# Loading the residual rows of x from SyncE instead of GpSimd, and widening a zero fill, in an attention-and-gate kernel

## Chip, cores, metric

The kernel runs on one core of one Trainium2 chip. The metric is device time in microseconds (us) of one launch, the median of several executions. Engines are named as the profile names them: PE is TensorE's matmuls, PEld its weight loads, DVE is VectorE, ACT is ScalarE, POOL is GpSimd, SP is SyncE; "SPq" or "ACTq" is the instruction queue of that engine, from which it also issues transfers. The landing of a transfer is the moment when its data is in place; PSUM is the memory that TensorE writes its results to. All runs here are recorded as of the same (fast) state; a "slow start" or "slow execution" below is something else, a matter of the first 10 us.

## The reference, cut to what matters

```
x  = A_x                                    # 2048 rows x 640, bf16
xn = layernorm(x)
q  = xn @ wq                                # 32 heads of 192
k, v = the last 512 rows of the caches
s  = softmax(q k^T / sqrt(192)) v @ wo      # 2048 x 640, summed over 32 heads
g  = silu((sigmoid(xn @ w_gate) * (xn @ w_up)) @ w_down)
return x + s * g
```

The kernel first computes the gate `g` and keeps it. Then it runs attention in 8 groups of 4 heads (0 to 7), each over four blocks ("units") of 512 rows, and sums the projections of the groups in `acc`. So that the end is cheap, `acc` is turned into `acc * g + x` already after group 6, on GpSimd; group 7 adds only its own part times `g`.

## The kernel before: the parts that count

The start: order of the first loads. The fill writes zeros that the gate-weight load then overwrites. It is a delay: ScalarE's load has to wait for it.

```
nc.vector.memset(wg_sb[:, 0, 0:2 * P], 0.0)      # 256 columns = 128 words of 32 bits
load_x(0, 1)                                     # SyncE, 160 KB
load_x(1, 1)                                     # SyncE, 160 KB
load_f(nc.scalar, wg_sb, wg_r, 0, 4, 0, 3)       # ScalarE, gate weights, 384 KB
load_f(nc.sync, wg_sb, wg_r, 0, 4, 3, NCD)       # SyncE, 256 KB
load_f(nc.sync, wu_sb, wu_r, 0, 4, 0, 3)         # SyncE, up weights, 384 KB
load_x(2, 1)
# ... cut: the rest of the loads
dummy(17)                                        # matmuls on zeros, to get TensorE going
```

The projection of one 128-row block, where the rows of x are loaded:

```
def project(u, q, k, out_eng=None, add=nc.vector, two=True):
    g, b = u // NB, u % NB                       # group, block of 512 rows
    t = b * TQ + q                               # block of 128 rows
    for turn in range(2 if two else 1):
        # ... cut: 12 matmuls of oT[u] and wo into a PSUM bank, then a yield
    # ... cut: groups 0 and 7
        nc.vector.tensor_tensor(cols(acc[:, t, :]), res, cols(acc[:, t, :]), ALU.add)
    if g == NG - 2:                              # group 6
        x_sb = fin.tile([P, D], BF16, name="row")            # pool fin has 2 buffers
        nc.gpsimd.dma_start(x_sb[:], xf[t * P:(t + 1) * P, :])
        nc.gpsimd.tensor_tensor(acc[:, t, :], acc[:, t, :], gate[:, t, :], ALU.mult)
        nc.gpsimd.tensor_tensor(acc[:, t, :], acc[:, t, :], x_sb[:], ALU.add)
    yield
```

The driver interleaves attention values of unit u with projections of unit u - 2. SyncE issues, in program order, the transposes of the next group's keys (`turn_keys`), those of each unit's output (`turn_out`, o_st to oT, four per unit) and the wo loads. GpSimd issues the loads of the next group's wq, keys and values (`load_values`, into the single tile `vbuf`).

The softmax here doesn't subtract the row's maximum and nothing guards it: scores larger than these inputs give would overflow.

## Time and profile before

| | before |
|---|---|
| time, 3 runs | 922.06 us (921.71 to 922.27) |
| TensorE busy | 914.1 of 919.2 us |
| GpSimd busy | 134.6 us |
| GpSimd waits for rows of x | 16.1 us in 14 waits |

The prediction below shows the busy table, TensorE's waits, the chain at the start and the two timelines.

### The profile page before, as it was taken

The numbers are of one execution on the slowest core, as the hardware profiler recorded it, in microseconds if no ns is written. First come the engines' busy times: TensorE is split into PE (matmuls) and PEld (weight loads), VectorE is DVE, ScalarE is ACT, GpSimd is POOL, SyncE is SP. The second block draws the span as 40 slices with busy tenths as digits, with TensorE's granted clock in tenths as the row PEclk, the third lists the DMA queues.
The fourth block names the chain that finished last, engine by engine and source line by source line (L and its number), as shares of the span: only waits on it lengthen the run. The fifth ranks groups of instructions, "written<-read, shape, count | busy, mean of one in ns | idle before, by whom it ended". The sixth has DMA issues, their size and how long they took to land.

```text
span 919.2 us, 24974 instructions
## 1 busy us (share of the span) xinstructions
PE 914.1 (99%) x11333; PEld 622.8 (68%) x11333; DVE 492.5 (54%) x989; ACT 302.3 (33%) x332; POOL 134.6 (15%) x159
## 2 busy tenths in 40 slices
PE   9999999999999999999999999999999999999998
PEld 4445455465868686867676777777776767686875
DVE  6462522444646464646555555545564646464667
ACT  4222222255141424242333333242424151515150
POOL 1000100001002000200020011001100111174733
PEclk9999999999999999999999999999999999999999
DMA  9820330115434334342425162515251615253435
GB/s 320 164 44 1 89 87 1 43 62 88 78 63 111 81 64 77 94 98 45 95 85 107 36 104 79 113 31 109 66 108 46 113 61 95 62 120 104 88 84 135
DMA packets 172106, 79.35 MB, mean 86 GB/s; under 512 B 149952, under 2 KB 167568, under 8 KB 172000
## 3 DMA queue, kind: packets, MB, share of 16 engines
q1 hardware_dynamic: 164640, 55.85, 31.1%
q0 software_dynamic: 5808, 20.52, 7.8%
q8 instruction: 88, 1.44, 0.7%
q10 hardware_dynamic: 1552, 1.39, 0.5%
q14 instruction: 18, 0.15, 0.1%
HBM read 39.45 MB, written 2.62 MB: 46 GB/s over the span
## 4 chain that ended last, share of the span: by engine, by line
PE 99%; DMA 1%; DVE 0%; SPq 0%; DVEq 0%; issue 0%
PE bank L517 22%; PE bank L446 21%; PE bank L468 19%; PE bank L428 18%; PE bank L251 8%; PE bank L263 6%; PE bank L293 3%; PE bank L394 1%; DMA wu_sb<-in_B_w_up_dram 1%; PE bank L552 0%; DVE o_sb L498 0%; DVE gate L503 0%; SPq L162 0%; PE bank L235 0%; SPq L167 0%; DVEq L654 0%
## 5 line engine op out<-in xcount | busy, mean ns | idle before, releaser
L432 ACT ACTIVATE E<-bank 128x1024 bf16<-128x1024 f32 x256 | 255.3, 1022 | 456.5 <-PE bank L428 456.4
L446 PE MATMUL bank<-xnT,wq_sb 64*128 64x512 bf16 x1800 | 226.4, 376 | 0.0
L517 PE MATMUL bank<-wo_sb,oT 64*128 64x320 bf16 x2688 | 205.2, 296 | 0.0
L428 PE MATMUL bank<-qT,kT 64*128 64x512 bf16 x1536 | 200.7, 376 | 0.0
L468 PE MATMUL bank<-vbuf,E 64*128 64x193 bf16 x4096 | 195.3, 243 | 0.0
L468 PEld LDWEIGHTS <-E 64*128 64x128 bf16 x4096 | 178.8, 94 | 10.2 <-issue 0.3
L517 PEld LDWEIGHTS <-oT 64*128 64x128 bf16 (+1 forms) x2892 | 163.2, 94 | 30.7 <-issue 0.3
L453 DVE CAST qT<-bank 128x1024 bf16<-128x1024 f32 x90 | 110.2, 1224 | 128.5 <-PE bank L446 128.5
L446 PEld LDWEIGHTS <-wq_sb 64*128 64x128 bf16 x1800 | 106.1, 100 | 87.0 <-issue 0.4
L428 PEld LDWEIGHTS <-kT 64*128 64x128 bf16 x1536 | 88.1, 94 | 73.5
L481 DVE TENSOR_TENSOR o_st<-bank,rden 128x768 bf16<-128x768 f32 x128 | 122.6, 957 | 4.4
L532 DVE TENSOR_TENSOR acc<-bank,acc 128x640 f32<-128x640 f32 x96 | 79.0, 823 | 20.2 <-PE bank L517 20.2
L118 POOL DMA_DIRECT2D vbuf<-in_A_v_cache_dram x28 | 21.1, 753 | 311.0 <-PE bank L468 308.1
L451 DVE COPY seen<-bank 128x2 f32<-128x2 f32 x90 | 14.3, 159 | 79.1 <-PE bank L446 79.1
L480 DVE RECIPROCAL rden<-bank 128x4 f32<-128x4 f32 x128 | 23.4, 182 | 60.6 <-PE bank L468 59.6
L263 PE MATMUL bank<-wd_sb,hT 128*128 128x512 bf16 (+1 forms) x384 | 52.8, 299 | 0.0
L263 PEld LDWEIGHTS <-hT 128*128 128x128 bf16 x384 | 29.7, 98 | 23.1
L251 PE MATMUL bank<-xnT,wg_sb 128*128 128x512 bf16 x180 | 44.7, 379 | 0.0
L251 PE MATMUL bank<-xnT,wu_sb 128*128 128x512 bf16 x180 | 44.7, 379 | 0.0
L257 DVE TENSOR_TENSOR hT<-bank,sig 128x512 bf16<-128x512 f32 x36 | 24.8, 690 | 37.1 <-ACT sig L254 37.1
L254 ACT ACTIVATE sig<-bank 128x512 bf16<-128x512 f32 x36 | 21.5, 597 | 55.8 <-PE bank L251 52.7
L97 POOL DMA_DIRECT2D wq_sb<-in_A_wq_dram x7 | 6.3, 900 | 210.7 <-PE bank L446 210.7
(51 smaller groups left out, 406.1 us busy)
## 6 DMA issues: line engine op xcount, KB each, us to landing
wo_sb<-in_A_wo_dram SPq DMA_DIRECT2D x7, 960.0 KB, 5.6
wq_sb<-in_A_wq_dram POOLq DMA_DIRECT2D x7, 960.0 KB, 6.1
k_st<-in_A_k_cache_dram POOLq DMA_DIRECT2D x14, 384.0 KB, 5.6
vbuf<-in_A_v_cache_dram POOLq DMA_DIRECT2D x28, 192.0 KB, 3.5
row<-in_A_x_dram POOLq DMA_DIRECT2D x16, 160.0 KB, 2.7
oT<-o_st SPq DMA_TRANSPOSE x128, 3.4
x_sb<-in_A_x_dram SPq DMA_DIRECT2D x3, 640.0 KB, 9.4
wd_sb<-in_B_w_down_dram SPq DMA_DIRECT2D x1, 1920.0 KB, 14.4
```

The lines of the kernel that those rows point to most:

```text
L251: nc.tensor.matmul(bank[k][:, half, 0:r1 - r0], lhsT=w[:, c, f * P:(f + 1) * P], rhs=xnT[:, b, c, r0:r1], start=(c == 0), stop=(c == NCD - 1))
L257: nc.vector.tensor_tensor(hT[b][:, f, r0:r1], bank[k][:, 1, 0:r1 - r0], sig[:, 0:r1 - r0], ALU.mult)
L263: nc.tensor.matmul(wide(k)[:, d0:d1], lhsT=hT[b][:, f, q * P:(q + 1) * P], rhs=wd_sb[:, f, d0:d1], start=(f == 0), stop=(f == NF - 1))
L293: nc.tensor.matmul(bank[k][:, half, :], lhsT=xcT[:, c, t * P:(t + 1) * P], rhs=w[:, c, fg * FT:(fg + 1) * FT], start=(c == 0), stop=(c == ...
L428: nc.tensor.matmul(bank[k][:, i, :], lhsT=kT[r, pr, j, c * P:(c + 1) * P], rhs=q[r, pr * DJ + j, :], start=(j == 0), stop=(j == DJ - 1))
L432: nc.scalar.activation(E[u, pr][:, c, :, :], bank[k][:], AF.Exp, scale=scale_qk)
L446: nc.tensor.matmul(bank[k][:, half, :], lhsT=wq[r, c, col:col + DJ * (P - 1) + 1:DJ], rhs=xnT[r, b, c, :], start=(c == 0 and not second), ...
L453: nc.vector.tensor_copy(qT[u][:, 2 * m:2 * m + 2, :], bank[k][:])
L468: nc.tensor.matmul(o4[:, q, 0:DH + 1], lhsT=e[r, c, h % 2, q * P:(q + 1) * P], rhs=vbuf[r, h, c, 0:DH + 1], start=(turn == 0 and qq == 0 a ...
L481: nc.vector.tensor_tensor(o_st[u][:, :, h * DH:(h + 1) * DH], o4[:, :, 0:DH], rden[:].to_broadcast([P, TQ, DH]), ALU.mult)
L517: nc.tensor.matmul(res[:, half, :], lhsT=oT[u][r, cc, q * P:(q + 1) * P], rhs=wo[r, cc, half * HD:(half + 1) * HD], start=(turn == 0 and c ...
L532: nc.vector.tensor_tensor(cols(acc[:, t, :]), res, cols(acc[:, t, :]), ALU.add)
```

## The change

Its intent: take 16 transfer issues off GpSimd and have each row in place before its sum is ready. The fill becomes 352 columns wide (176 words), so the gate-weight load starts a little later and leaves the x rows alone a little longer.

```
-        nc.vector.memset(wg_sb[:, 0, 0:2 * P], 0.0)
+        nc.vector.memset(wg_sb[:, 0, 0:352], 0.0)
...
         res = bank[k][:, :, 0:HD]
+        if g == NG - 2:
+            x_sb = fin.tile([P, D], BF16, name="row")
+            nc.sync.dma_start(x_sb[:], xf[t * P:(t + 1) * P, :])
         for turn in range(2 if two else 1):
...
         if g == NG - 2:
-            x_sb = fin.tile([P, D], BF16, name="row")
-            nc.gpsimd.dma_start(x_sb[:], xf[t * P:(t + 1) * P, :])
             nc.gpsimd.tensor_tensor(acc[:, t, :], acc[:, t, :], gate[:, t, :], ALU.mult)
```

## The prediction

> **What bounds the kernel now.** I read the busy table first, then who waited for whom on TensorE, then the chain of waits at both ends, then the timelines of GpSimd and SyncE around the rows of x.
>
> ```profile
> PE 914.1 (99%) x11333; PEld 622.8 (68%) x11333; DVE 492.5 (54%) x989; ACT 302.3 (33%) x332; POOL 134.6 (15%) x159
> ```
> ```profile
> PE bank L194 <- DVE warm L169: 1.1, 1, 1.1
> PE bank L293 <- DMA wg_sb<-in_B_w_gate_dram: 0.2, 1, 0.2
> ```
>
> TensorE is busy for 914.1 of 919.2 us and its only two recorded waits (line, what it waited for, us in total, times, longest) are both in the first 6 us. Granted clock is 1.0 throughout. In every 20 us stretch from 20 to 900 us that I asked for, TensorE is busy for all 20. So a change that leaves TensorE's instructions alone can gain only in two places: the start, or the drain after the last matmul at 915 us. It can lose wherever it makes something late that TensorE needs.
>
> The start, from the chain that ended last (start us, us, what):
>
> ```profile
> 1.66 0.43 SPq L167
> 2.09 0.04 issue
> 2.13 4.96 DMA wu_sb<-in_B_w_up_dram
> 7.10 0.04 issue
> 7.14 2.53 PE bank L293 x11
> ```
>
> The up weights, issued by SyncE at 2.13, land at 7.09, and all later work hangs on them. The four rows of GpSimd and the six of SyncE below (start us, us, engine) show the stretch that the move touches:
>
> ```profile
> 801.88 1.39 POOL L536 TENSOR_TENSOR acc<-acc,gate 128x640 f32<-128x640 f32 x1 [37.76 <-DVE acc L532]
> 803.36 1.40 POOL L537 TENSOR_TENSOR acc<-acc,row 128x640 f32<-128x640 f32 x1
> 804.70 0.58 POOL L535 DMA_DIRECT2D row<-in_A_x_dram  x1
> ...
> 834.89 3.02 POOL L118 DMA_DIRECT2D vbuf<-in_A_v_cache_dram  x4
> ```
> ```profile
> 780.26 0.58 SPq L130 DMA_DIRECT2D wo_sb<-in_A_wo_dram  x1
> 797.37 12.10 SPq L137 DMA_TRANSPOSE kT<-k_perm  x8
> 809.86 16.88 SPq L490 DMA_TRANSPOSE oT<-o_st  x8
> 843.06 0.37 SPq L130 DMA_DIRECT2D wo_last<-in_A_wo_dram  x1
> 856.88 17.10 SPq L490 DMA_TRANSPOSE oT<-o_st  x8
> 874.40 7.96 SPq L504 DMA_DIRECT2D out_dram<-gate  x4
> ```
>
> GpSimd multiplies a group-6 sum by the gate and adds a row of x, 16 times in two batches of 8; each row is fetched on its own queue just before. SyncE, where the fetch goes, is in the same stretch busy with transposes, first of the last group's keys, then of the attention output oT.
>
> **What the Trainium skill says.** (1) "DMA: Bandwidth & Descriptors", section "Anatomy of one DMA — SWDGE (gpsimd) path": engines that carry a DMA do not wait on semaphores; the wait is on the issuing sequencer. The SyncE waits agree: transposes L490 stood 330 us behind o_st. Hence a row load that waits for a free buffer holds up every transpose behind it. (2) Same page, "SWDGE vs HWDGE vs iDMA": a DMA issued from GpSimd has its descriptors written in software there, one from SyncE in hardware. Agrees with 577 ns of GpSimd (POOL) busy time per row. (3) "SBUF — State Buffer", "Who interferes with whom": a VectorE instruction with one SBUF input does not contend with GpSimd. Agrees: the sum L532 (one input in PSUM) took 814 to 826 ns in all 96 cases, with GpSimd busy or idle. So taking work off GpSimd frees nothing on VectorE here.
>
> **The change, part by part.**
>
> *Removed from GpSimd:* 16 issues x 0.577 = 9.2 us (busy 134.6 to about 125.4). The 16.1 us that L537 waited for rows is not simply gone, see below. None of this stands before a matmul.
>
> *Added to SyncE:* 16 issues at about 0.45 us (the early x rows of the same 160 KB took 0.40 to 0.48) = 7 us, plus waits for one of two row buffers. The instruction order of the changed kernel puts them as: 8 key transposes, 4 rows, 4 oT transposes, 4 rows, 4 oT transposes, last wo, and again 4, 4, 4, 4. "Ahead of the projection" in the program is therefore not early in time: the first row stands behind the key transposes, which end at 809.5, while before it was fetched at 763.5. I step it through with multiply 1.4, add 1.4, issue 0.45, landing 2.7 us (the rows' median before).
>
> Batch one. Rows 0, 1 issue at 809.5 and 810, land at 812.2 and 812.7. Add 0, at 803.4 before, starts at 812.2 (a new wait of 8.8 us) and frees its buffer at 813.6; row 2 goes out then. Multiply and add 1 end at 816.4, row 3 goes out. Only now, at 816.9, do the oT transposes start, 7 us later than 809.86; four take about 6.1 us, to 823, the last landing near 826. TensorE needs them at 844.81 (next projection): slack 18 us. Rows 4, 5 at 823 land at 825.7; adds 4 and 5 end at 827.1 and 829.9, and free rows 6 and 7. The second set of transposes starts at 830.4 (821.5 before) and lands by 839, needed near 856: slack 17 us. Add 7 ends at 835.5, so the value loads of the last group start there, against 834.89: 0.6 us later. The four issue in 3.0 us and land 3.9 us after issue, the last near 842.5; TensorE first reads them here:
>
> ```profile
> 844.15 0.84 PE L468 MATMUL bank<-vbuf,E 64*128 64x193 bf16 x16
> ...
> 868.50 0.99 PE L517 MATMUL bank<-wo_last,oT 64*128 64x320 bf16 x12
> ```
>
> Slack about 1.7 us for all four, over 4 us for the first head: the tightest place on GpSimd's side.
>
> Batch two. Last wo at 843.06; rows 8, 9 at 843.5 and 844, landed by 846.7, before GpSimd's multiply at 848.9. Adds 8 and 9 end at 851.7 and 854.6, so rows 10, 11 issue by 855.05. The oT transposes become ready at 856.6 (start at 856.88 before): not delayed, with 1.5 us to spare. They must have landed for the matmul at 868.50 above; before, the last of them issued by 863 and landed near 867. So this chain has some 3 us before TensorE would stall: the tightest place on SyncE. Rows 12 and 13 issue behind them at 863 and land at 865.7; adds 12 to 15 end by about 875.5, against 885.2 before. The last set of transposes waits for rows 14, 15 until 870.4, about 2 us late, and is needed near 894.9.
>
> Sum for the move: GpSimd's waits for rows become fewer and longer (8.8 + 2.3 + 3.6, about 15 us in place of 16.1), its work ends 10 us earlier, and TensorE moves by 0. GpSimd then idles until 898.59 anyway, when the last products arrive.
>
> *Zero fill 352 wide.* Its values are overwritten; it is a delay, since ScalarE's first gate-weight DMA waits for it (L172, 165 ns). It becomes 176 words instead of 128: 48 more. An estimate from the two early fills: 128 words in 165 ns, 1 word in 59, so 106/127 = 0.83 ns a word, 0.04 us more. The gate weights start 0.04 us later and leave the DMA engines to the first x rows for that long. The up weights (landing 7.09) queue behind the same bytes either way (1344 KB with x rows 0 and 1); their landing may move by 0.05 either way. TensorE's own path to that matmul, x row, normalise, transpose, ends at 7.06, so an earlier x row cannot gain more than the up weights allow. Net -0.1 to +0.1 us.
>
> Total: 922.06 + 0 (move) - 0.1 to + 0.1 (fill). I take 921.9, a shade under, because the fill looks tuned by trial; that is a choice, not a derivation.
>
> **Rivals.** *A: SyncE blocks.* Row loads that wait for buffers stand ahead of the transposes. If landings take 5 us (the slowest row before) instead of 2.7, or GpSimd runs behind, batch two eats its 3 us and TensorE stalls at 868.50 for 1 to 2 us, once: 923 to 924. For it: two buffers only, and oT's order behind the rows. Against: batch two has rows 8 and 9 in hand early. *B: the value loads come late.* Batch one ends later than worked out by over 2 us and TensorE waits at 844.15: up to 1 us more. For: three round trips in a row. Against: later heads are read some 3 us apart. *C: the move pays.* Freed GpSimd time shortens something on the path: 1 us or more less. For: 9.2 us of issues gone. Against: no TensorE wait there to remove, and VectorE undisturbed. *D: the start gains more* because the x rows come first: at most the 0.2 us wait on gate weights and a little of the 4.96 us transfer.
>
> **Range and chances.** The three runs before span 0.56 us. Down: the start offers at most some 0.3 us, and noise as much: 921.1. Up: rivals A or B for about 1 us, perhaps one chance in eight: 923.0. Two per cent is 18 us; nothing here is of that size, and only a stall repeated for every row would be: faster 0.005, same 0.985, slower 0.01.
>
> **What would show it.** Right: TensorE's waits still only those at the start; 16 fewer GpSimd instructions and 9 us less busy; add 0 starting near 812; first oT transposes near 817 rather than 809.86; value loads near 835; the wo_last matmul still near 868.5; transfer of the up weights landing within 0.1 us of 7.09. Wrong: a TensorE gap at 844 or 868, an earlier end of the whole chain between 760 and 890, or a start shifted by over 0.3 us.

## More of the kernel before

One more view of the kernel before is needed, four lines of the transfers (what, by whom, how often, KB each, median us from issue to landing):

```profile
row<-in_A_x_dram POOLq DMA_DIRECT2D x16, 160.0 KB, 2.7
oT<-o_st SPq DMA_TRANSPOSE x128, 3.4
wg_sb<-in_B_w_gate_dram ACTq DMA_DIRECT2D x1, 384.0 KB, 4.0
wu_sb<-in_B_w_up_dram SPq DMA_DIRECT2D x1, 384.0 KB, 5.0
```

Add an issue time to the last column and you have the landing: the gate weights, issued at 1.18, land at 5.2 us after the start.

## The result, and the profile after

The changed kernel took 921.38 us (4 runs, 921.10 to 921.56), the kernel before in the same rounds 921.89 us (4 runs, 921.71 to 922.27). The ratio is 0.9994, with a 95% interval of 0.9976 to 1.0011: the same. Ratios here are the mean time of one kernel's fast runs over that of the other's of the same rounds, so not quite the ratio of the medians quoted.

Busy table and TensorE's waits (line, what it waited for, us, times, longest) of the changed kernel:

```profile
PE 913.3 (99%) x11314; PEld 623.0 (68%) x11333; DVE 493.0 (54%) x989; ACT 302.4 (33%) x332; POOL 125.7 (14%) x143
```
```profile
PE bank L194 <- DVE warm L169: 1.1, 1, 1.1
PE bank L293 <- DMA wg_sb<-in_B_w_gate_dram: 0.2, 1, 0.2
```

GpSimd has 16 instructions and 8.9 us less (a few matmul records are missing from the trace, so PE's x11314 is not a change of the program). TensorE's waits are the two of before. The chain that ended last, at the start:

```profile
2.13 5.26 DMA wu_sb<-in_B_w_up_dram
7.40 0.04 issue
7.44 2.53 PE bank L293 x11
```

In this execution the up weights landed at 7.39 instead of 7.09, and TensorE's first use of them stands at 7.44 instead of 7.14. That 0.30 us is the whole difference between the two profiled spans (919.5 and 919.2): nothing is gained or lost afterwards. GpSimd and SyncE around the moved rows:

```profile
802.19 1.39 POOL L537 TENSOR_TENSOR acc<-acc,gate 128x640 f32<-128x640 f32 x1 [38.38 <-DVE acc L535]
812.51 1.40 POOL L538 TENSOR_TENSOR acc<-acc,row 128x640 f32<-128x640 f32 x1 [8.93 <-DMA row<-in_A_x_dram]
...
826.22 1.40 POOL L538 TENSOR_TENSOR acc<-acc,row 128x640 f32<-128x640 f32 x1 [2.43 <-DMA row<-in_A_x_dram]
...
836.07 3.02 POOL L118 DMA_DIRECT2D vbuf<-in_A_v_cache_dram  x4
...
865.93 1.40 POOL L538 TENSOR_TENSOR acc<-acc,row 128x640 f32<-128x640 f32 x1 [3.48 <-DMA row<-in_A_x_dram]
```
```profile
797.68 12.24 SPq L137 DMA_TRANSPOSE kT<-k_perm  x8
809.97 7.14 SPq L514 DMA_DIRECT2D row<-in_A_x_dram  x4
817.21 6.34 SPq L490 DMA_TRANSPOSE oT<-o_st  x4
823.65 7.15 SPq L514 DMA_DIRECT2D row<-in_A_x_dram  x4
830.91 5.91 SPq L490 DMA_TRANSPOSE oT<-o_st  x4
843.37 0.39 SPq L130 DMA_DIRECT2D wo_last<-in_A_wo_dram  x1
843.86 11.54 SPq L514 DMA_DIRECT2D row<-in_A_x_dram  x4
857.18 6.08 SPq L490 DMA_TRANSPOSE oT<-o_st  x4
863.36 7.17 SPq L514 DMA_DIRECT2D row<-in_A_x_dram  x4
870.63 5.20 SPq L490 DMA_TRANSPOSE oT<-o_st  x4
```

The time of the waits did not vanish: 14 short waits for rows (16.1 us) became three long ones, 8.93 + 2.43 + 3.48 = 14.8 us. The rows stand behind the key transposes, and the oT transposes stand behind the rows, 7.35 us later than before in the first set. TensorE sees none of it:

```profile
844.45 0.85 PE L468 MATMUL bank<-vbuf,E 64*128 64x193 bf16 x16
...
868.81 0.99 PE L520 MATMUL bank<-wo_last,oT 64*128 64x320 bf16 x12
```

Both stand 0.30 to 0.31 us later than before, the shift of the start, and there is no wait in brackets behind them.

### The profile page after: what moved, and what is told of

The parts are those of the page before. It is cut to its first block, busy times and chain, and to the rows that moved or that the text cites. A ratio compares the mean times of both kernels' runs of the same rounds, so it can differ in the third digit from the quotient of the medians.

```text
span 919.5 us, 24969 instructions
## 1 busy us (share of the span) xinstructions
PE 913.3 (99%) x11314; PEld 623.0 (68%) x11333; DVE 493.0 (54%) x989; ACT 302.4 (33%) x332; POOL 125.7 (14%) x143
## 4 chain that ended last, share of the span: by engine, by line
PE 98%; DMA 1%; DVE 0%; issue 0%; SPq 0%; DVEq 0%
PE bank L520 22%; PE bank L446 21%; PE bank L468 19%; PE bank L428 18%; PE bank L251 8%; PE bank L263 6%; PE bank L293 3%; PE bank L394 1%; DMA wu_sb<-in_B_w_up_dram 1%; PE bank L553 0%; DVE o_sb L498 0%; DVE gate L503 0%; SPq L162 0%; PE bank L235 0%; SPq L167 0%
## 5 line engine op out<-in xcount | busy, mean ns | idle before, releaser
L263 PE MATMUL bank<-wd_sb,hT 128*128 128x128 bf16 (+1 forms) x377 | 52.4, 298 | 0.4
L110 POOL COPY k_perm<-k_st 128x768 bf16<-128x768 bf16 x32 | 25.5, 827 | 75.0 <-DMA k_st<-in_A_k_cache_dram 75.0
```

The lines of the kernel that those rows point to most:

```text
L110: nc.gpsimd.tensor_copy(kp[:, pr, :, :, i * H2:(i + 1) * H2], kst[:, i, :, :].rearrange("p c (i j) -> p c j i", j=DJ),)
L263: nc.tensor.matmul(wide(k)[:, d0:d1], lhsT=hT[b][:, f, q * P:(q + 1) * P], rhs=wd_sb[:, f, d0:d1], start=(f == 0), stop=(f == NF - 1))
```

## The experiments

Theory 1, that of the prediction: neither part is worth anything that can be measured, and the 0.5 us between the medians is spread of the start. Rivals: the fill makes it (theory 2), the move makes it (theory 3). Ten kernels, twelve runs.

**Nothing changed, timed against itself.** No edit.

> The kernel before, unchanged, timed against itself. It shows what the timing resolves and how much the start moves from execution to execution. All theories: ratio 1.000; I expect the medians within 0.3 us of each other and the landing of the up weights in the profile to differ from 7.09 us by up to 0.3 us, as it did between the two profiles in hand (7.09 and 7.39).

Measured: 921.52 us (921.42 to 921.82) against 921.65 us for before (9 runs, 921.12 to 922.50); ratio 0.9998, 0.9984 to 1.0011. Up weights landed at 7.25. So a single comparison of a few runs resolves about 0.13% (1.2 us), and one program's executions spread over 1.4 us.

**The fill alone.**

```
-        nc.vector.memset(wg_sb[:, 0, 0:2 * P], 0.0)
+        nc.vector.memset(wg_sb[:, 0, 0:352], 0.0)
```

> Only the zero fill is 352 wide, rows stay on GpSimd. Theory 1 (both parts are worth nothing that can be measured): within 0.3 us of before, ratio 0.9997 to 1.0003. Theory 2 (the fill makes the 0.5 us between the medians in hand): 0.4 to 0.6 us faster than before, with the up weights landing earlier than in the null run. Theory 3 (the move makes it): as theory 1 here.

Measured: 921.62 us (921.23 to 922.26), ratio 0.9998, 0.9986 to 1.0011. Theory 2's gain of 0.4 to 0.6 us in the medians is not there.

**The move alone.** The diff of the change without its first hunk.

> Only the rows move to SyncE, the fill stays 256 wide. Theory 1: within 0.3 us of before, TensorE's idle time after the first 8 us unchanged, GpSimd busy about 125.7 us, value loads issued near 836 us. Theory 2: as theory 1 here. Theory 3: 0.4 to 0.6 us faster, with a gain that shows between 760 and 890 us.

Measured: 921.58 us (921.06 to 921.76), ratio 0.9997, 0.9984 to 1.0009. GpSimd busy 125.4 us, row waits 14.9 us in three, value loads at 835.48. Theory 3's gain is not there either, and nothing differs between 760 and 890 us on TensorE.

**Both parts, on the same chip.**

> The changed kernel again, on the same chip as its parts. Theory 1: within 0.3 us of the null run. Theories 2 and 3: 0.4 to 0.6 us faster than the null run, as the part that makes it.

Measured: 921.66 us, ratio 1.0001, 0.9988 to 1.0013. So the 0.5 us of the first comparison does not come back: theory 1. But one of the five executions, the profiled one, took 923.35 us. TensorE at its start (start us, us, engine, what, how many; in brackets the wait before):

```profile
4.66 0.53 PE L235 MATMUL bank<-ident,xn 128*128 128x128 bf16 x3
6.14 0.58 PE L293 MATMUL bank<-wg_sb,xnT 128*128 128x512 bf16 x1 [0.95 <-DMA wg_sb<-in_B_w_gate_dram]
6.52 0.42 PE L235 MATMUL bank<-ident,xn 128*128 128x128 bf16 x2
6.73 1.91 PE L293 MATMUL bank<-wg_sb,xnT 128*128 128x512 bf16 x4
8.44 0.74 PE L235 MATMUL bank<-ident,xn 128*128 128x128 bf16 x5
8.97 1.31 PE L293 MATMUL bank<-wu_sb,xnT 128*128 128x512 bf16 x3
```

and the same stretch in the kernel before:

```profile
4.54 0.48 PE L235 MATMUL bank<-ident,xn 128*128 128x128 bf16 x3
5.21 0.38 PE L293 MATMUL bank<-wg_sb,xnT 128*128 128x512 bf16 x1 [0.19 <-DMA wg_sb<-in_B_w_gate_dram]
5.43 0.27 PE L235 MATMUL bank<-ident,xn 128*128 128x128 bf16 x2
5.54 1.24 PE L293 MATMUL bank<-wg_sb,xnT 128*128 128x512 bf16 x4
6.62 0.44 PE L235 MATMUL bank<-ident,xn 128*128 128x128 bf16 x5
7.14 0.81 PE L293 MATMUL bank<-wu_sb,xnT 128*128 128x512 bf16 x3
```

Two things are off. The gate weights landed at 6.10 instead of 5.2, so TensorE waited 0.95 us. And its matmuls are slow until about 9.8 us: four of the same form take 1.91 us instead of 1.24. The first use of the up weights comes at 8.97, while they had landed at 7.3 (2.13 + 5.2); with the three slow matmuls there (1.31 for 0.81) the delay against before is 1.83 + 0.50 = 2.3 us, as is the span's (921.6 against 919.2, 2.4). This is a second way for the start to go that the prediction did not foresee (TensorE had lost 2.34 us by 10.12, and the same 2.33 at 35 us); the next experiments are about it and about the move's slack.

**One row buffer instead of two**, on top of the change, to make the cost of a wrong order visible.

```
-            x_sb = fin.tile([P, D], BF16, name="row")
+            x_sb = fin.tile([P, D], BF16, name="row", bufs=1)
```

> The changed kernel with one row buffer in place of two, so that each of the 16 row loads waits for the add before it. My step model with the numbers of the changed kernel's profile (issue 0.35, landing 2.4, add 1.4, so 3.9 us a row): add 7 of batch one ends at 844.0 instead of 836.1, the value loads go out there, the first lands at about 847.9, and TensorE, which wants it at 844.45, stalls for 3.4 us once; the oT transposes are late by 3 to 10 us but still in time. Time 925.3 (921.9 + 3.4); 927.6 if TensorE waits for all four value loads. Rival A (SyncE blocks TensorE): the gap is at the first wo_last matmul (868.8 in the changed kernel) instead of at 844. Rival (row loads and value loads are hidden anyway): no gap, 921.4 to 922.3.

Measured: 926.18 us (925.14 to 926.37), ratio 1.0048, 1.0035 to 1.0061. GpSimd and TensorE of this kernel:

```profile
841.66 1.40 POOL L538 TENSOR_TENSOR acc<-acc,row 128x640 f32<-128x640 f32 x1 [1.02 <-DMA row<-in_A_x_dram]
843.00 3.02 POOL L118 DMA_DIRECT2D vbuf<-in_A_v_cache_dram  x4
```
```profile
843.35 1.48 PE L428 MATMUL bank<-qT,kT 64*128 64x512 bf16 x12
848.01 0.84 PE L468 MATMUL bank<-vbuf,E 64*128 64x193 bf16 x16 [3.18 <-DMA vbuf<-in_A_v_cache_dram]
...
872.63 0.98 PE L520 MATMUL bank<-wo_last,oT 64*128 64x320 bf16 x12
```

The value loads go out at 843.00 (7 us later than with two buffers), the first lands 5.0 us after its issue, and TensorE stands 3.18 us: rival B of the prediction, where the step model put it, and for the first head's load alone. That 3.18 comes so near to the expected 3.4 is partly luck: the loads went out 1.0 us earlier than the model's 844.0, and the first took 1.1 us longer than its 3.9. Rival A did not happen: SyncE began the oT transposes of the second batch at 865.18, 8.0 us later than in the changed kernel, and TensorE still reached the wo_last matmul without a wait, 3.8 us later. Of the 4.5 us in time, the profiled execution (925.14) has 3.5; the other three took about 1 us more, which no trace here shows. (Their mean granted clock is recorded as 0.998, that of the profiled one as 0.999; 0.998 is also what the profiled execution of the widest fill below has, with its stretch at half clock. So slow matmuls after the stall are a candidate, not shown.)

**Four row buffers**, on top of the change.

```
-            x_sb = fin.tile([P, D], BF16, name="row")
+            x_sb = fin.tile([P, D], BF16, name="row", bufs=4)
```

> The changed kernel with four row buffers: the four rows of a block are in flight at once and SyncE waits for no buffer within a block. My theory: add 0 still at 812.5 (SyncE is busy with key transposes until 810), oT transposes start at about 811.7 instead of 817.2, value loads at about 834 instead of 836.07, and TensorE gains nothing: within 0.3 us of before. Rival C (freeing GpSimd and SyncE pays): faster by 0.5 us or more.

Measured: 921.76 us (921.48 to 922.23), ratio 1.0003, 0.9990 to 1.0016. The oT transposes began at 811.71 and the value loads went out at 833.44. So SyncE's blocking within a batch can be taken away and TensorE gains nothing: the slack that the change used up was slack.

**No fill at all**, in the kernel before.

```
-        nc.vector.memset(wg_sb[:, 0, 0:2 * P], 0.0)
```

> The kernel before without the zero fill, so ScalarE's gate-weight load goes out about 0.45 us earlier (near 0.72 in place of 1.18), beside the x rows. If the fill is a delay that helps x, the first row of x lands later than 3.05 us and TensorE's first transpose starts later than 4.54; the up weights land at 7.1 to 7.4 as before. Theory 1: time within 0.3 us of before. Rival (the order of x and gate weights is worth something): 0.3 to 0.8 us slower.

Measured: 921.80 us (921.69 to 922.40), ratio 1.0004, 0.9992 to 1.0016. The gate-weight load went out at 0.74, and the first x row reached VectorE at 3.50 instead of 3.07 to 3.20 in the kernel before. The fill does what it is for, and the time does not show it.

**A fill of 1536 columns (768 words).**

```
-        nc.vector.memset(wg_sb[:, 0, 0:2 * P], 0.0)
+        nc.vector.memset(wg_sb[:, 0, 0:F], 0.0)
```

> The kernel before with the zero fill 1536 wide (768 words). From 0.165 us for 128 words and 0.20 for 176 I expect 0.6 us, so the gate-weight load goes out near 1.65 in place of 1.18, ten times the delay of the change. Then the gate weights land some 0.3 to 0.5 us later, TensorE's wait for them grows from 0.2 to 0.4 to 0.7 us, and its own path, 7.06 before, passes the landing of the up weights: 0.3 to 0.5 us slower. Rival (a longer delay keeps helping x): 0.3 us or more faster.

Measured: 925.52 us; five of six executions between 924.58 and 926.11, one at 921.99; ratio 1.0036, 1.0025 to 1.0048. My 0.3 to 0.5 us was ten times too small. The gate weights, issued 0.67 us later than before (1.85), landed 2.5 us later (7.68). And then TensorE ran slowly. The columns of the next view are the stretch, its length, busy us of PE, PEld, DVE, ACT and POOL, then the granted TensorE clock, the DMA share and GB/s:

```profile
6.00:8.00 2.00, 0.27 (x3) 0.15 (x3) 0.63 (x4) 0.00 (x0) 1.09 (x2) 1.00 1.08 362
8.00:10.00 2.00, 1.96 (x13) 1.00 (x12) 1.14 (x4) 0.74 (x2) 0.00 (x0) 0.79 1.08 352
10.00:12.00 2.00, 2.00 (x6) 0.76 (x5) 1.93 (x8) 0.41 (x2) 0.55 (x1) 0.50 1.09 350
12.00:14.00 2.00, 2.00 (x12) 0.96 (x12) 0.18 (x2) 0.49 (x1) 0.55 (x1) 0.85 1.09 347
```

Between 10 and 12 us TensorE is "busy" for all of 2.00 us with 6 matmuls, and the granted clock is 0.50. A 512-column matmul takes 634 ns there and 379 ns at other times. TensorE in the same stretch:

```profile
7.73 0.38 PE L293 MATMUL bank<-wg_sb,xnT 128*128 128x512 bf16 x1 [2.54 <-DMA wg_sb<-in_B_w_gate_dram]
...
8.05 1.24 PE L293 MATMUL bank<-wg_sb,xnT 128*128 128x512 bf16 x4
...
9.62 1.49 PE L293 MATMUL bank<-wu_sb,xnT 128*128 128x512 bf16 x3
10.90 2.08 PE L293 MATMUL bank<-wg_sb,xnT 128*128 128x512 bf16 x5
```

The first matmuls behind the pause still ran at full speed (four in 1.24 us, as in the kernel before); the slow ones came later. An estimate from the clock column: if the clock is either 1.00 or 0.50, the readings 0.79, 0.50 and 0.85 make 0.84 + 2.00 + 0.60 = 3.4 us at half speed. The wait is paid for twice: 2.5 us of standing, and more in the slow stretch behind it. The Trainium skill describes this: "TensorE: Matmul & The Clock Gate", section "What's actually happening", says that TensorE runs at half rate until it has been busy for a window of about 3.4 us, falls back after an idle one, and that the window runs freely, so that the moment of the switch varies from run to run. This trace agrees as to the factor (0.50) and the length of the slow stretch (the estimate of 3.4 us); that a whole idle window is needed for the fall it does not bear out, since the pause ahead of it was 2.54 us.

**A fill of 704 columns (352 words).** As above with `0:704`.

> The kernel before with a fill of 704 columns (352 words), between the change's 176 words and the 768 of the wide run. From 0.20 us for 176 words and 0.71 for 768 the fill takes 0.35 us, so the gate-weight load goes out near 1.39. Theory from the wide run (the x row gains nothing beyond the 256-column fill, while the gate weights land later and TensorE waits and then runs slow for a while): x still seen by VectorE at 3.1 us, gate weights landing 5.6 to 6.6, time 0.3 to 2 us above before and less steady. Rival (only the extreme width hurts, a threshold): within 0.3 us of before.

Measured: 924.40 us; three of four executions between 924.35 and 924.49, one at 921.99; ratio 1.0022, 1.0008 to 1.0037. The gate-weight load went out at 1.42 and landed at 6.15; TensorE waited 1.01 us and its next matmuls took 634 ns until about 9.8 us. The x row came at 3.12, no earlier than with 256 columns. The rival (a threshold far out) falls: under 0.25 us of delay is enough.

**The up weights issued by ScalarE**, in the kernel before, to see whether the transfer that the chain names can be brought forward.

```
-        load_f(nc.sync, wu_sb, wu_r, 0, 4, 0, 3)
+        load_f(nc.scalar, wu_sb, wu_r, 0, 4, 0, 3)
```

> The kernel before, with the first up-weight load issued by ScalarE behind its gate load instead of by SyncE as its fourth, so it goes out near 1.66 in place of 2.13. Theory that the up weights set the start: they land 0.2 to 0.4 us earlier than 7.1 to 7.5 and the time falls by 0.1 to 0.3 us (TensorE's own path, 7.06 to 7.3, allows no more). Rival (the same bytes through the same 16 engines land when they land, or the gate weights pay for it): no change, or the gate weights land later and the time rises by 0.3 us or more.

Measured: 923.58 us (922.60 to 924.81), ratio 1.0023, 1.0010 to 1.0036: slower, and the rival was right in kind. The up weights were issued at 1.67 and took 7.2 us, landing near 8.9. SyncE's 256 KB of the gate weights, also issued at 1.67, landed at 7.83 (6.16 us; 4.3 in the kernel before), and TensorE waited 1.60 us for them. Its next two matmuls still ran at 379 ns, the ones after them did not: the clock column reads 0.58 from 8 to 10 us and 0.56 from 10 to 12, by the same estimate 3.4 us at half speed. The Trainium skill, "DMA: Bandwidth & Descriptors", section "Issuing engines are not separate DMA queues", says that transfers from different issuing engines run on the same 16 DMA engines and interleave; that fits, but why an earlier issue lands later no run here tests.

**The changed kernel once more**, for its spread.

> The changed kernel once more, for the spread: one of nine executions so far stood at 923.35 with the gate weights landing at 6.1 instead of 5.2 to 5.5. If the 352-column fill makes that likely, one or two of five again exceed 922.6, which none of 24 executions of before did; if it was chance, none does. Median within 0.3 us of before in either case.

Measured: 922.62 us; 921.49, 921.57, 923.67 and 923.91; ratio 1.0012, 0.9999 to 1.0025. Two of four are slow. The profiled one (921.49) is instructive:

```profile
5.91 0.38 PE L293 MATMUL bank<-wg_sb,xnT 128*128 128x512 bf16 x1 [0.85 <-DMA wg_sb<-in_B_w_gate_dram]
...
6.24 1.25 PE L293 MATMUL bank<-wg_sb,xnT 128*128 128x512 bf16 x4
```

TensorE waited 0.85 us for the gate weights (5.87), yet its matmuls ran at 379 ns. The dummy matmuls ahead tell why: here they fell from 421 to 272 ns before 4 us, so TensorE was up to speed before the pause. In the slow execution above they still took 421 ns at 4.4 us, and the pause came before it was up to speed. So in these traces a pause of about 1 us (0.95, and 1.01 with 704 columns) went with a slow start where the switch to full speed had not happened yet, and one of 0.85 us did no harm where it had. That is not the only way: the pauses of 2.54 us (widest fill) and 1.60 us (up weights on ScalarE) were followed by matmuls at full speed, and TensorE fell back to half speed after them. The two slow executions of this run have no trace.

**The fill alone once more**, for its spread.

> The 352-column fill alone once more, for its spread. So far executions above 922.6 us: none of 40 with a fill of 256 columns or none, 3 of 23 with 352 (all three with the rows moved as well), 3 of 4 with 704, 5 of 6 with 1536. If the fill alone makes the slow starts, about one in eight executions is above 923, so with five the chance to see one or more is about one half, and an execution above 923 here would settle it for the fill alone; if the slow starts need the moved rows too, none is above 922.6. Median within 0.3 us of before in both.

Measured, on another chip: 921.68 us (921.53 to 922.39), ratio 0.9997, 0.9984 to 1.0011. No slow execution, which leaves open what it was meant to settle.

All executions together, by the width of the fill (the run with one row buffer and the one with the up weights on ScalarE left out; gate, x and up are from the profiled executions, up from issue and time to landing):

| fill, words | gate load issued | gate landed | first x row at VectorE | up landed | executions over 923 us |
|---|---|---|---|---|---|
| none | 0.74 | 4.5 | 3.50 | 7.7 | 0 of 5 |
| 128 | 1.18 to 1.19 | 5.1 to 5.2 | 3.07 to 3.20 | 7.1 to 7.5 | 0 of 44 |
| 176 | 1.23 to 1.24 | 5.1 to 6.1 | 3.09 to 3.14 | 7.1 to 7.6 | 3 of 28 |
| 352 | 1.42 | 6.15 | 3.12 | 7.6 | 3 of 4 |
| 768 | 1.85 | 7.68 | 3.10 | 8.3 | 5 of 6 |

## Why the prediction was right, point by point

*TensorE is the bound, and the change cannot reach it.* Right. Its waits are the same two. The two parts alone (0.9998 and 0.9997), both together (1.0001) and even four row buffers (1.0003) are all the kernel before within what the timing resolves.

*The move, stepped through on SyncE and GpSimd.* Right in every position. Add 0 at 812.2 predicted, 812.51 measured; first oT transposes 816.9, 817.21; second 830.4, 830.91; value loads 835.5, 836.07; last transposes 870.4, 870.63; the second batch's transposes not delayed (857.18 is 856.88 plus the shift of the start). Waits for rows 8.8, 2.3 and 3.6 us predicted, 8.93, 2.43 and 3.48 measured. GpSimd busy 125.4 predicted, 125.7 measured. Two terms were a little off and do not matter to the sum: a row's issue took 0.35 us, not 0.45, and landed 2.4 us after it, not 2.7. The order of instructions on each queue, not the place in the source, gave all this: the load that the source puts "ahead" began 46 us later than before (809.97 against 763.55).

*The tightest places.* Half right. On GpSimd's side the value loads are indeed what TensorE meets first, shown by the stall of 3.18 us with one row buffer. On SyncE's side "some 3 us before TensorE would stall" was too careful: with one buffer the transposes came 8.0 us late against a TensorE that was 3.8 us late, and it did not wait.

*Rivals.* A and B did not occur in the changed kernel; B occurs when a buffer is taken away. C (the move pays) was tried by the move alone and by four buffers, and falls. D (the start gains because the x rows come first) falls: between 128 and 768 words the first x row comes at 3.1 to 3.2 whatever the fill.

*The fill's size.* 0.04 us more predicted; 205 against 165 ns measured. Right.

*"All later work hangs on" the up weights, and the fill is worth -0.1 to +0.1 us.* The sum held for the medians (921.62 against 921.65 and 921.68 against 921.67), but the step behind it is incomplete. The up weights and the gate weights are two near-equal bounds: in the profiles of the fill alone and of two of three of the changed kernel the chain at the start hangs on the gate weights. With 0.04 to 0.06 us of later issue the landing came 0 to 0.9 us later, and where TensorE was not yet up to speed, the latest landing (6.10) went with 2 us of time; whether the later issue is its cause stays open (below). The prediction allowed for a stall of that size in the middle of the kernel, not at its start.

*The skill, point (3).* The page's sentence has a condition that the prediction left out, that the instruction is outside VectorE's two-port performance modes. The conclusion stands on the trace: the 96 sums took 814 to 826 ns before and after.

*The 0.5 us that the first comparison showed.* The prediction's 921.9 leaned "a shade under" on a guess about tuning. The four-run medians seemed to confirm it; the kernels side by side on one chip do not (921.66 both, 921.65 before), and the profiled spans point the other way.

*The test at the start.* The changed kernel failed it: the up weights landed at 7.39, not "within 0.1 us of 7.09". The test was too tight, not the change to blame: the kernel before itself gave 7.25 in another execution, the move alone, with the old fill, 7.46.

**What stays open.** Whether the 352-column fill makes slow starts more likely than 256. For it: 3 of 28 against 0 of 49 with 256 or none, the wait and the slow matmuls seen in one of the slow ones, and a clear effect at 704 and 1536. Against: all three were of the kernel with the rows moved too, none of ten with the fill alone. The slow execution with a trace had lost its time by 10.12 us, long before the moved rows. More executions of the fill alone would settle it. Why the gate weights land so much later for a slightly later issue is open too, and so is the last microsecond of the run with one row buffer.

## What to carry to other kernels

Moving work off an engine that no one waits for gains nothing, however large its waits look; follow each queue in its own program order, add up issue, landing and buffer release, and compare with the moment when the busy engine needs the result. If a change is worth less than the spread of the start, time its parts against an unchanged copy on the same chip, and look at single executions, not only at medians: a short wait while TensorE is still getting up to speed can cost more in the slow stretch that follows than in the wait itself.

## What the Trainium skill lacked or had wrong

- "DMA: Bandwidth & Descriptors" has no figure for how far a small shift between the two hardware queues moves a landing: the same 384 KB from ScalarE, issued at 1.18, 1.42 and 1.85 us beside SyncE's loads, landed at 5.2, 6.15 and 7.68 us.
- The same page fits a transfer's time for the GpSimd path only; here 160 KB took 2.7 us issued from GpSimd and 2.4 us from SyncE (medians of 16).
- "TensorE: Matmul & The Clock Gate" has TensorE fall back to half rate after an idle window of about 3.4 us. Here pauses of 1.60 and 2.54 us were enough: half speed followed, for 3.4 us by the estimate above. Shorter pauses mattered during the warm-up: those of 0.95 and 1.01 us went along with matmuls at 631 to 634 ns (379 at full speed) until about 9.8 us, while one of 0.85 us after the switch to full speed did no harm.
- The same page warns that the clock events of a trace have been seen to be unreliable, but not that the slow stretch before the first switch is missing: between 8 and 10 us the granted clock read 1.00 in the slow execution of the changed kernel, while matmuls took 631 ns. The later fall of the widest fill it did show (0.50).
